# Regrouping a fused linear-attention and FFN kernel, with two more units transposed by DMA

## The chip, the cores and the metric

One core of one Trainium2 chip. The time is device microseconds (us) of one execution, median of several runs; the kernel before takes 233.85 us. A profile's span is about 2 us shorter than that time, because it starts with the first instruction and ends with the last.

In the lines of the profile PE is TensorE (PEld its weight loads), DVE is VectorE, ACT ScalarE, POOL GpSimd, and SPq SyncE's queue, which issues nearly all transfers.

## The reference, cut to what matters

A block-wise decaying linear attention over 4 batches, 8 heads, 768 positions and head width 64, and then a bilinear feed-forward network on its output, 3072 tokens wide 512:

```python
intra = einsum('bhic,bhjc->bhij', qb, kb) * Dmask;  intra = einsum('bhij,bhjd->bhid', intra, vb)
inter = einsum('bhid,bhde->bhie', qb * lam_pow, kv_state)
out[:, :, sl] = intra + inter
kv_state = lam_block * kv_state + einsum('bhsd,bhse->bhde', kb * rev_pow, vb)
# ... then, with x = out as (tokens, heads * width):
y = ((x @ w_a) * (x @ w_b)) @ w_out          # 512 -> 1536 -> 512, float32 out
```

## The kernel before

The 3072 tokens are 24 units of 128 tokens, and six units make a batch. Units are handled in groups. While TensorE runs the feed-forward matmuls of one group, the attention of later units is fitted between them by a hand-written plan: `PLAN[g]` lists pieces by slot. Slots 0 to 11 of a group are after each pair of projection halves, slots from 12 on after each half of a unit's output matmuls.

```python
GROUPS = (4, 1, 2, 4, 4, 4, 4, 1)
LOOKAHEAD = (3, 2)
DMA_T_FROM = 9                       # from this unit on q and k are transposed by DMA, before it on TensorE
PLAN = { ...
    2: [(0, "V", 6), (1, "T", 7), (1, "P", 8), (4, "T", 8), (4, "P", 9), (6, "S", 7),
        (6, "S", 8), (7, "V", 7), (6, "P", 10), (10, "V", 8),
        (12, "Q", (7, 8, 9, 10)), (12, "P", 11), (13, "V", 9), (14, "P", 12),
        (14, "O2", (9, 10))], ... }
```

The pieces: P prepares a unit (scales k and q on GpSimd, casts v, issues later loads), T transposes it on TensorE, S is scores and masks, V is the state update, O2 the outputs of two units, and Q the outputs of two units with the scores of two others between them. W stores a kept output: the outputs of the first seven units wait in SBUF and are stored later.

```python
    def prep_k(u):
        make_ks(u, "dve" if u < n0 + 2 else "pool")
        make_qs(u, "pool")
        used["u"] = u + 1
        if u >= DMA_T_FROM:
            qkT = qkT_pool.tile([128, 2, HP, 128], BF16, name="qkT", tag="qkT")
            nc.sync.dma_start_transpose(out=..., in_=...)          # cut
    def prep_v(u):
        make_vb(u, "pool" if u < n0 + 3 else "dve")
        pump()                                                     # issues the next loads, same queue
    def pieces_O(us, nxt=()):
        kqs = [score_banks() for u in nxt]
        for u in us: inter(u)
        for u, kq in zip(nxt, kqs): scores(u, kq)
        for u in us:
            intra(u); xT, col = xTs[u]; evac_o(u, xT, col)
        # ... state update beside, then masks(u, kq) on VectorE for each of nxt
```

The FFN of one group, with the special end of the very last unit, whose output goes out in three pieces:

```python
        for f in range(FC):
            a_sb = a_part(f, xT, gt)        # 4 matmuls of 128 * units columns, evicted by ScalarE
            b_part(f, xT, gt, a_sb, ab)     # 4 more; VectorE multiplies out of PSUM
            hook(f)
        for t in range(n):
            if last and t == n - 1:
                for lo, hi in ((0, 256), (256, 384), (384, 512)): ...   # out_mms, store of each piece
                return
            # out_mms in two halves with hooks, store(u0 + t, ...)
```

At the start TensorE runs idle matmuls, `warm(13, 512)`: 13 of 512 columns.

## Time and profile before

| | before |
|---|---|
| time, median of 5 | 233.85 us (233.6 to 234.01) |
| span of the profiled run | 231.8 us |
| first projection matmul to last matmul, TensorE | 209.88 us |
| last matmul's start to the end of the span | 3.31 us |

In the chain of waits a piece is "start, length, what"; when neighbouring pieces on TensorE (PE) touch, it issued without a hole. From 18.6 to 228.5 us that is so but for one wait of 0.34 us near 51 us. The lines are in the prediction. To add up TensorE's time I also took the start-to-start distance of every pair of neighbouring matmuls and subtracted the issue time of its kind (216, 109 and 56 ns for 512, 256 and 128 columns, 28.5 and 14.5 ns for the narrow attention kinds); what is left over is a wait or a mode switch (about 0.1 us, where TensorE goes between matmuls that use its whole array and the attention matmuls that use half of its rows or columns).

### The profile page before, as it was taken

How to read it: one execution, taken by the hardware profiler on the slowest of the kernel's cores; microseconds unless marked ns; L12 is line 12 of the kernel's file. 1: busy time of each engine (PE TensorE's matmuls, PEld its weight loads, DVE VectorE, ACT ScalarE, POOL GpSimd, SP SyncE). 2: the span in 40 equal slices, each digit the busy share in tenths (PEclk: the TensorE clock that was granted, in tenths of full speed). 3: DMA queues.
4: the chain of work that ended last, by engine and by line, in shares of the span. 5: the costliest groups of instructions: out<-in, count | busy, mean ns of one | idle time of the engine just before them, and what ended most of it. 6: DMA issues, size and time to landing. Idle time of an engine off the chain costs nothing.

```text
span 231.8 us, 4520 instructions
## 1 busy us (share of the span) xinstructions
PE 225.2 (97%) x1775; PEld 124.6 (54%) x1775; DVE 115.9 (50%) x204; ACT 91.1 (39%) x172; POOL 50.6 (22%) x65
## 2 busy tenths in 40 slices
PE   7799999999999999999999999999999999999994
PEld 2474444449698554454544454544454544444494
DVE  0896566636469726684334484235583323332050
ACT  3585754066463342333233332333332233332251
POOL 6070000248373333445000543001200000000000
PEclk9999999999999999999999999999999999999999
DMA  4999999999999999998759997229300220000311
GB/s 151 303 283 351 348 364 293 295 207 223 185 225 176 224 208 209 209 197 190 270 189 200 220 182 121 91 96 205 65 3 0 91 93 0 1 0 5 130 49 48
DMA packets 96389, 38.84 MB, mean 168 GB/s; under 512 B 83312, under 2 KB 91888, under 8 KB 96368
## 3 DMA queue, kind: packets, MB, share of 16 engines
q1 hardware_dynamic: 96224, 38.54, 72.9%
q8 instruction: 14, 0.23, 0.4%
q14 instruction: 7, 0.06, 0.1%
q10 hardware_dynamic: 144, 0.00, 0.0%
HBM read 28.32 MB, written 6.29 MB: 149 GB/s over the span
## 4 chain that ended last, share of the span: by engine, by line
PE 92%; DMA 3%; ACT 2%; SPq 1%; DVE 0%; issue 0%
PE a_ps L435 27%; PE b_ps L435 27%; PE op L467 27%; DMA k<-in_k_dram 3%; PE o_ps L352 3%; PE kq L310 2%; PE o_ps L342 2%; PE kvd L366 2%; PE tps L296 1%; ACT o_kept L458 1%; SPq L209 1%; PE kq L578 1%; ACT xT L359 0%; PE kv L366 0%; PE tk L542 0%; DVE scratch L531 0%
## 5 line engine op out<-in xcount | busy, mean ns | idle before, releaser
L447 DVE TENSOR_TENSOR ab<-a_sb,b_ps 128x512 bf16<-128x512 bf16 (+2 forms) x96 | 52.3, 552 | 77.9 <-PE b_ps L435 56.9
L435 PE MATMUL a_ps<-xT,wa_sb 128*128 128x512 bf16 (+2 forms) x384 | 77.2, 326 | 0.6 <-ACT xT L359 0.6
L435 PE MATMUL b_ps<-xT,wb_sb 128*128 128x512 bf16 (+2 forms) x384 | 77.2, 326 | 0.0
L442 ACT CAST a_sb<-a_ps 128x512 bf16<-128x512 f32 (+2 forms) x96 | 45.6, 481 | 63.1 <-PE a_ps L435 61.5
L467 PE MATMUL op<-wo_sb,ab 128*128 128x512 bf16 (+2 forms) x312 | 65.6, 363 | 0.0
L435 PEld LDWEIGHTS <-wb_sb 128*128 128x128 bf16 x384 | 34.5, 98 | 28.7
L435 PEld LDWEIGHTS <-wa_sb 128*128 128x128 bf16 x384 | 33.7, 98 | 29.1 <-POOL wa_sb L162 0.6
L467 PEld LDWEIGHTS <-ab 128*128 128x128 bf16 x312 | 28.8, 98 | 29.9
L327 DVE TENSOR_TENSOR m<-kq,lotri 128x512 bf16<-128x512 f32 x47 | 29.3, 682 | 18.1 <-PE kq L310 17.8
L259 POOL TENSOR_TENSOR qk<-kf,lp_k 128x512 bf16<-128x512 f32 x18 | 18.9, 1049 | 74.7 <-DMA kf<-in_k_dram 47.3
L264 POOL TENSOR_TENSOR qk<-qf,lp_q 128x512 bf16<-128x512 f32 x20 | 22.0, 1099 | 23.4 <-DMA qf<-in_q_dram 23.4
L462 ACT COPY o_sb<-op 128x512 f32<-128x512 f32 (+2 forms) x19 | 10.3, 541 | 34.0 <-PE op L467 34.0
L359 ACT CAST xT<-o_ps 128x512 bf16<-128x512 f32 x22 | 12.0, 590 | 17.9 <-PE o_ps L352 17.5
L398 DVE TENSOR_TENSOR st<-kvd,bdiag 128x512 bf16<-128x512 f32 x18 | 12.3, 682 | 4.9 <-PE kvd L366 3.8
L273 DVE CAST vb<-vf 128x512 bf16<-128x512 f32 x17 | 9.4, 553 | 0.0
L298 ACT COPY qkT<-tps 128x1024 bf16<-128x1024 bf16 x5 | 5.1, 1012 | 9.9 <-PE tps L296 9.9
L197 PE MATMUL idle<-idle_sb 128*128 128x128 bf16 (+1 forms) x31 | 7.2, 372 | 1.3 <-DVE idle_sb L192 1.3
L352 PE MATMUL o_ps<-m,vb 128*64 128x128 bf16 x192 | 7.9, 222 | 0.0
L273 POOL CAST vb<-vf 128x512 bf16<-128x512 f32 x7 | 4.7, 666 | 14.0 <-DMA vf<-in_v_dram 14.0
L342 PEld LDWEIGHTS <-st 128*128 128x128 bf16 x80 | 5.4, 98 | 2.8
L310 PE MATMUL kq<-qkT 64*128 64x128 bf16 x160 | 6.6, 218 | 0.0
L352 PEld LDWEIGHTS <-vb 128*64 128x64 bf16 x192 | 5.8, 109 | 1.4
(57 smaller groups left out, 87.4 us busy)
## 6 DMA issues: line engine op xcount, KB each, us to landing
vf<-in_v_dram SPq DMA_DIRECT2D x24, 256.0 KB, 4.9
qf<-in_q_dram SPq DMA_DIRECT2D x20, 256.0 KB, 4.4
kf<-in_k_dram SPq DMA_DIRECT2D x20, 256.0 KB, 4.6
out_dram<-o_sb SPq DMA_DIRECT2D x16, 256.0 KB, 2.0
wst<-in_moe_w_a_dram SPq DMA_DIRECT2D x6, 512.0 KB, 8.7
wst<-in_moe_w_b_dram SPq DMA_DIRECT2D x6, 512.0 KB, 8.8
wst<-in_moe_w_out_dram SPq DMA_DIRECT2D x6, 512.0 KB, 8.5
out_dram<-o_kept SPq DMA_DIRECT2D x7, 256.0 KB, 2.5
```

Source lines behind the costliest of these rows:

```text
L259: eng_of(eng).tensor_mul(qk[:, 1], raw.pop((u, "k")), lp_k[:, u % NB].to_broadcast([128, H, D]))
L264: eng_of(eng).tensor_mul(U[u]["qk"][:, 0], raw.pop((u, "q")), lp_q[:, u % NB].to_broadcast([128, H, D]))
L273: eng_of(eng).tensor_copy(vb, vf)
L310: nc.tensor.matmul(kq[i][:, hp, :], lhsT=d["kT"][p, hp, :], rhs=d["qT"][p, hp, :], start=True, stop=True, skip_group_check=True)
L327: nc.vector.tensor_mul(m, kq[i], lotri_bc)
L352: nc.tensor.matmul(d["o"][p, hp, :], lhsT=d["vb"][:, 2 * hp + i, :], rhs=d["m"](i, hp), start=(first and hp == 0), stop=True, skip_group_c ...
L359: nc.scalar.copy(xT[:, :, col:col + BLK], o_ps)
L398: nc.vector.tensor_mul(st[:].rearrange("p hp i d -> p hp (i d)"), ps[:].rearrange("p hp i d -> p hp (i d)"), bdiag_bc)
L435: nc.tensor.matmul(ps[:, :gt], lhsT=w_sb[:, s, f * 128:(f + 1) * 128], rhs=xT[:, s, :gt], start=(s == 0), stop=(s == KS - 1))
L442: nc.scalar.copy(a_sb[:, :gt], ps[:, :gt])
L447: nc.vector.tensor_mul(ab[:, f, :gt], a_sb[:, :gt], ps[:, :gt])
L467: nc.tensor.matmul(op[:, lo:hi], lhsT=ab[:, f, t * 128:(t + 1) * 128], rhs=wo_sb[:, f, lo:hi], start=(f == 0), stop=(f == FC - 1))
```

## The change

The intent: the early groups are made smaller, so that fewer units have to be ready early, while transfers are scarce. That makes room to transpose units 7 and 8 by DMA and take 16 transposes off TensorE. Kept outputs of the first seven units are stored a group later. The diff, cut to its core:

```diff
-GROUPS = (4, 1, 2, 4, 4, 4, 4, 1)
+GROUPS = (4, 1, 2, 2, 4, 4, 4, 3)
-DMA_T_FROM = 9
+DMA_T_FROM = 7
@@ PLAN
-    2: [(0, "V", 6), (1, "T", 7), (1, "P", 8), (4, "T", 8), (4, "P", 9), (6, "S", 7), ... cut
+    2: [(0, "V", 6), (1, "P", 8), (4, "P", 9), (9, "P", 10), (10, "S", 7), (10, "S", 8),
+        (11, "V", 7), (13, "P", 11), (14, "O2", (7, 8)), (15, "P", 12)],
+    3: [(1, "S", 9), (1, "S", 10), (2, "V", 9), (5, "Q", (9, 10, 11, 12)), (6, "P", 13),
+        (8, "V", 11), (9, "P", 14), (12, "O2", (11, 12))],
-PLAN[3] += [(_s, "W", None) for _s in range(12, 19)]
+PLAN[4] += [(_s, "W", None) for _s in range(9, 16)]
-PLAN[6] = [(4, "O", 23)]
+PLAN[6] = [(1, "P", 23), (4, "V", 21), (7, "Q", (21, 22, 23)), (12, "O", 23)]
-    qkT_pool = ctx.enter_context(tc.tile_pool(name="qkT", bufs=5))
+    qkT_pool = ctx.enter_context(tc.tile_pool(name="qkT", bufs=6))
-            elif c >= used["u"] + LOOKAHEAD[used["u"] > 9]:
+            elif c >= used["u"] + LOOKAHEAD[used["u"] > 8]:
... cut: the plans of the four-unit groups move by two units, the state update of unit 8 in 64-column form
```

## The prediction

> **What bounds the kernel now.** I read four views of the kernel before, in this order: the page's busy shares and slices, the chain of waits, the groups of instructions by form, and the DMA issues with the timeline of the transfer queue. The page first:
>
> ```profile
> span 231.8 us, 4520 instructions
> PE 225.2 (97%) x1775; PEld 124.6 (54%) x1775; DVE 115.9 (50%) x204; ACT 91.1 (39%) x172; POOL 50.6 (22%) x65
> DMA  4999999999999999998759997229300220000311
> ```
>
> PE is busy 97% of the span, DVE and ACT half or less. The DMA row is the second thing to see: nearly full for the first 18 of 40 slices (some 104 us), then slack. A busy PE need not be a full one, so I went to the chain of waits, whose pieces are PE start to start:
>
> ```profile
> by line: PE a_ps L435 31.9%; PE b_ps L435 29.0%; PE op L467 20.9%; PE kq L310 5.5%; PE o_ps L352 3.8%; PE kvd L366 3.0%; PE tps L296 3.0%; PE o_ps L342 3.0%; PE kvd L387 0.4%
> 67.38 0.44 PE b_ps L435 x4
> 67.81 0.45 PE tps L296 x8
> 68.26 0.44 PE a_ps L435 x4
> ...
> 70.01 0.55 PE kq L310 x16
> ...
> 84.69 0.86 PE b_ps L435 x4
> ```
>
> This window (62 to 92 us) covers what the change touches, and its chain names nothing but PE: each piece starts where the last one ends. Four 512-column matmuls take 0.86 us, four 256-column ones 0.44, and in the last group four 128-column ones:
>
> ```profile
> 220.68 0.22 PE a_ps L435 x4
> 226.04 2.66 PE op L467 x36
> ```
>
> So 216, 109 and 56 ns each: 53.3 ns per 128 columns plus about 2.5. The same chain between 46 and 62 us shows the one wait after the start that costs something, where group 1's first matmul waits for ACT's eviction of xT (group table: a_ps 0.5 us idle, released by ACT xT). From 52 to 226 us PE issues without a hole. The end is 11.3 us of a one-unit group, whose last output goes out in three pieces.
>
> **What the Trainium skill says.** "TensorE: Matmul & The Clock Gate", section "Back-to-back issue gap", gives N/2.4 + 2.5 ns for a warm matmul, which is 56, 109 and 216 ns here; it adds that in a real stream N=128 takes about 81 ns and N=512 about 131. This trace agrees with the formula (56, 109, 216) and not with those two figures. "TensorEngine Tiling (Array Packing)", section "Key Properties", says that changing the tiling mode drains TensorE. The trace shows it: the first matmul after a block of 64-row or 64-column matmuls is late by some 0.1 us (a_ps at 70.56 takes 0.54 in place of 0.44), so a scores block costs two such switches. "DMA: Bandwidth & Descriptors", section "Issuing engines are not separate DMA queues", says that all transfers run on the same 16 engines and interleave. So a DMA transpose competes with loads, and I read its cost from the transfers' landing times in the trace. "Perfetto Trace Analysis", section "Identifying the Most-Contended Engine", calls matmul busy time a bad metric because matmuls are pipelined; hence the start-to-start reading above.
>
> **The change part by part.**
>
> Regrouping, (4,1,2,4,4,4,4,1) to (4,1,2,2,4,4,4,3). The number of groups stays 8, so the weights of the two projections are run over 8 times in both: 96 matmuls per group, 12 wide output matmuls per unit. Only widths change: a 4-unit and a 1-unit group become a 2 and a 3. Per matmul 216 + 56 = 272 ns before. A 384-column matmul should take 160 + 2.5 = 162.5 ns (estimate from the three measured widths), and 162.5 + 109 = 271.5. Times 96, the gain is 0.05 us: nothing. One might have expected the one-unit group to be inefficient, but at 56 ns it isn't: PE needs 0.45 us per pair of halves, ACT 0.27 and DVE 0.29, and its 96 matmuls take 5.36 us without a hole. The tail is the same three pieces.
>
> Units 7 and 8 transposed by DMA. This removes 16 PE transposes at 56 ns: two pieces of 0.45, so 0.90 us off the path, every bit of it on PE's chain (the two tps pieces at 64.75 and 67.81). It also removes two ACT copies of 1.01 us, which are off the path (ACT 39% busy).
>
> Attention pieces in another order. From unit 7 on, before has 2 separate score pairs, 7 combined pieces with scores, one output pair and one single; after has 3, 6, 2 and 1. With switches of 96 + 120 = 0.22 us per score pair, 96 + 118 + 122 = 0.34 per combined piece, and 0.22 per output piece: before 0.43 + 2.35 + 0.44 = 3.22, after 0.65 + 2.02 + 0.65 = 3.32, so +0.10. The state update of unit 8 now runs in 64-column form: 0.12 in place of 0.22 (the pieces at 82.30 and 79.76), so -0.10. PE's instructions go from 1775 to 1763: minus 16, plus 4. Sum of these two: 0.
>
> Later stores of the 7 kept outputs: ordinary 256 KB stores, 2.5 us to landing, in a stretch where the DMA row has slack. Nothing on the path.
>
> One more transpose buffer and the earlier switch of the load lookahead from 3 to 2 units only serve the supply. Net of PE's own work: -0.05 - 0.90 + 0 = **about -0.95 us**, to 232.9.
>
> What may be given back is supply. Before, units 7 to 10 were all needed while the first two-unit group ran, to 83.8 us. After, that group has only 7 and 8 to prepare, and I add its length: 12 x 0.872 for the projections, 5.18 for 24 output matmuls, 0.66 for scores, 2 x 0.22 for state, 1.23 for outputs, so 18.0 us from 62.4 to 80.4. The next two-unit group then wants units 11 and 12 in its sixth slot: 80.4 + 6 x 0.872 + 0.66 + 0.22 = 86.5 us, and the transposed unit 12 after another 0.9, at some 87.4.
>
> When does unit 12 land? In the saturated stretch a load lands 1.2 us after the one before, a transpose about 0.9, and a load just behind a transpose about 1.5. Before, it landed at 86.1, having waited for POOL: its queue entry stood until POOL's product was ready.
>
> ```profile
> 68.19 4.64 SPq L282 DMA_TRANSPOSE qkT<-qk  x2
> ...
> 80.19 2.01 SPq L282 DMA_TRANSPOSE qkT<-qk  x1
> ```
>
> The waits of the queue itself say the same in sum (total, times, longest):
>
> ```profile
> SPq L282 <- POOL qk L264: 5.5, 7, 2.7
> ```
>
> After, the order of the queue is unit 9's v (lands 64.7 as before), transpose 7, loads of 10, transposes 8 and 9, loads of 11, transpose 10, loads of 12, transpose 11, loads of 13, transpose 12. That is 12 loads and 6 transposes: 8 x 1.2 + 4 x 1.5 + 6 x 0.9 = 21.0, so 85.7 at the earliest, and 87 to 88 if POOL's product (two products of 1.05 us after the load of k at about 79, so 81.1) or the queue's 2.1 us of issue holds it. Against 87.4 that is a wait of 0 to 0.6 us.
>
> A second small debt lies beside it. Four masks (2.47 us of DVE) now fall in slot 1 of a two-unit group, and the combined piece comes four slots later, not in the output phase. DVE after scores at 82.8: masks to 85.2, product 2 to 85.6, state copy to 86.2, products 3 and 4 to 87.0. The combined piece's output bank is the one that product 4 reads (of seven banks in turn), and PE arrives at 86.5: about 0.45 us of waiting. The two waits overlap. I put **+0.4 us** on both.
>
> Sum: 233.85 - 0.95 + 0.4 = **233.3 us**.
>
> **The rivals.** (a) No wait at all: all of 0.95 arrives, 232.9. For it: PE's queue had no hole before with a similar DVE load (four masks in slot 6, with no wait), and the regrouping spreads the demand. Against it: the 0.45 us worked out above. (b) The DMA supply fails by more: two further transposes in the full stretch push unit 12, or unit 11's v that DVE casts in order, several us late, and PE stands: 235 or more. For it: the DMA row at 9, and POOL's 47 us of waiting for k. Against it: most of POOL's waiting comes from running ahead, and the demand has been moved later. If units 13 on slid as well, they have 20 us in hand: their scores come at 107. (c) The smaller last group pays by a shorter tail, or a wider one by a better rate: some us. The rate of 56 ns at 128 columns speaks against it, and the tail is the same in both. (d) DVE becomes the bound in the two-unit groups: it was busy 14.8 of 21.4 us in the first one; after, the two together hold about the same work in 37 us. It speaks against.
>
> **Range and chances.** Best case is all of the PE saving and a little of the wait at 51.2 us: 232.5. A wait of 1.5 us makes 234.4. So 232.5 to 234.4 should hold 8 times in 10. Over 2% faster (under 229.2) would need five times what I find: 2%. Over 2% slower (over 238.5) needs a wait of 5 us: 3%. Within 2%: 95%.
>
> **What would show it.** In the profile after: transposes on PE 24 in place of 40; a 384-column form at some 162 ns start to start (four in 0.65 us in the chain); first 256-column matmul near 62.4 and the second two-unit group near 80.4; a hole of about 0.4 us on PE near 86.5, released by DVE's product or by the transpose into qkT; the last group from about 205 with the same three-piece end. I am wrong if the time moves by more than 1.5 us, if PE shows a hole of over 1 us past 52 us, if 384 columns cost other than 160 to 165 ns, or if the last group shows waits for ACT or DVE.

## The result, and the profile after

The changed kernel took 234.5 us (233.83 to 234.97, 5 runs). A ratio here is the mean time of one kernel's fast runs over that of the other's fast runs of the same rounds, so not quite the ratio of the medians. It was 1.0028 with a 95% interval of 1.0008 to 1.0048: slower by 0.3%, where a gain of 0.2% had been forecast, and just outside the range. The profile shown next is that of the slowest of the five runs (234.97), so its losses are larger than those of the median run; e12 gives a second profile.

The page of the changed kernel, same lines as before:

```profile
span 233.1 us, 4467 instructions
PE 222.7 (96%) x1742; PEld 127.7 (55%) x1763; DVE 116.6 (50%) x204; ACT 89.2 (38%) x170; POOL 50.2 (22%) x65
DMA  4999999999999999999999639990231000220012
```

The weight loads (PEld) count 1763, as foreseen; 21 matmul records are missing from the trace. TensorE's busy time fell by 2.5 us, in part because of those missing records, and the span rose by 1.3. The DMA row stays full to slice 22 (some 128 us) in place of slice 18.

The 384-column matmuls of the last group, in the chain of waits (start, length):

```profile
205.66 0.65 PE a_ps L433 x4
```

Four in 0.65 us are 162.5 ns each, as estimated. Up to 82 us TensorE keeps the forecast to 0.2 us: the first two-unit group starts at 62.5 us and the second at 80.55 (forecast 62.4 and 80.4). Then it leaves it. The chain of waits from 79 to 90 us:

```profile
76.80 4.50 DMA kf<-in_k_dram
...
81.46 1.04 POOL qk L257
82.50 1.19 POOL qk L262
...
83.71 5.06 DMA qkT<-qk
...
88.81 0.40 PE kq L308 x8
```

For the first time past the start the chain runs through a transfer. Unit 12's k lands at 81.3 us (I had reckoned 79), GpSimd makes its two products, the transpose is issued at 83.7 and lands at 88.77 (reckoned: 85.7 at the earliest, 87 to 88 likely), and only then can TensorE start the last eight scores. VectorE (DVE) in the same stretch, with the idle time before an instruction and what ended it in brackets:

```profile
82.32 0.47 DVE L271 CAST vb<-vf 128x512 bf16<-128x512 f32 x1 [2.27 <-DMA vf<-in_v_dram]
...
83.37 2.47 DVE L325 TENSOR_TENSOR m<-kq,lotri 128x512 bf16<-128x512 f32 x4
...
86.69 1.07 DVE L445 TENSOR_TENSOR ab<-a_sb,b_ps 128x256 bf16<-128x256 bf16 x3
```

It stood 2.27 us before the cast of unit 12's v, with the next group's products behind that cast in its queue. Then came four masks in one block, and products 3, 4 and 5 only at 86.7. What TensorE waited for in 62 to 100 us (total, times, longest; the idle time here leaves out the drain of the pipeline, so start to start it is 0.22, 0.60 and 0.58 us):

```profile
PE o_ps L340 <- DVE ab L445: 0.4, 1, 0.4
...
PE kq L308 <- DMA qkT<-qk: 0.4, 1, 0.4
PE a_ps L433 <- DVE ab L445: 0.2, 1, 0.2
```

The sums from start to start, in us, from the first projection matmul to the last matmul:

| | before | after | after minus before |
|---|---|---|---|
| feed-forward matmuls | 187.11 | 187.06 | -0.05 |
| transposes on TensorE | 2.24 | 1.34 | -0.90 |
| attention matmuls | 16.12 | 16.01 | -0.11 |
| mode switches, waits, rounding | 4.41 | 5.94 | +1.53 |
| sum | 209.88 | 210.35 | +0.47 |
| last matmul's start to the end | 3.31 | 4.26 | +0.95 |

The own work fell by 1.06, or 0.96 with one more switch; the waits near 82 to 89 us took 1.4 back. The rest, 0.95, is not on TensorE at all. It comes after the last matmul. The output stores from 226 us on, before (first line: issue times of the queue; second: from issue to landing, least, median, most):

```profile
L463 SPq DMA_DIRECT2D out_dram<-o_sb x3: 332/382/603, 227.8 to 229.0; - x3
...
DMA to landing us min/median/max: 1.7/1.8/2.0
```

and after:

```profile
L461 SPq DMA_DIRECT2D out_dram<-o_sb x4: 332/358/1537, 227.1 to 230.4; - x4
...
DMA to landing us min/median/max: 1.7/3.4/4.3
```

There is one store more at the end, the 256 KB of unit 22, issued at 227.08. It took 4.35 us to land, and the pieces behind it, issued at 228.18 and 228.75, took 3.5 and 3.2. In the trace's packet records something stands beside them (my table, not a view of the profile):

```
packets near the end (start us, bytes, ns)        before                     after
instruction fetch, one 16384 B packet             227.62  16384   945        228.19  16384  1714
unit 22's first 120 store packets, 2048 B each    -                          227.91 to 228.65, 81 to 93 ns each
unit 22's last 8 store packets                    -                          229.90 231 | 230.11 227 | 230.32 186 | 230.51 to 230.83, 84 to 85 each
```

Of the store's 128 packets 120 were through by 228.75. The last eight, a sixteenth of them, came from 229.90 on, when the fetch's packet ended (228.19 + 1.71). A first explanation: they are the share of one of the 16 DMA engines, and queued there behind the fetch. The packet records shown do not name the engine, so at this point it is a guess; it is tested below.

How this reaches the end of the program: the queue took 1.54 us to issue the third of these four stores (0.33 us in e5, where nothing is late). So the last piece, whose copy was done at 229.44, was issued at 230.38, 0.94 us later, and landed 1.73 us after that, as it does elsewhere. That is nearly all of the 0.95. Why the queue was held is not shown; the long issue ended at 230.28, 0.37 us after the fetch's packet.

### The profile page after: what moved, and what is told of

It is laid out like the page before. It is cut to its first block, busy times and chain, and to the rows that moved or that the text cites. A ratio compares the mean times of both kernels' runs of the same rounds, so it can differ in the third digit from the quotient of the medians.

```text
span 233.1 us, 4467 instructions
## 1 busy us (share of the span) xinstructions
PE 222.7 (96%) x1742; PEld 127.7 (55%) x1763; DVE 116.6 (50%) x204; ACT 89.2 (38%) x170; POOL 50.2 (22%) x65
## 4 chain that ended last, share of the span: by engine, by line
PE 85%; DMA 7%; SPq 2%; ACT 1%; issue 1%; POOL 1%; DVE 0%; POOLq 0%; ACTq 0%
PE a_ps L433 26%; PE b_ps L433 25%; PE op L465 24%; DMA k<-in_k_dram 3%; PE o_ps L350 3%; DMA qkT<-qk 2%; PE kq L308 2%; DMA kf<-in_k_dram 2%; PE o_ps L340 2%; PE kvd L364 1%; SPq L280 1%; ACT o_kept L456 1%; SPq L207 1%; PE tps L294 1%; POOL qk L262 1%
## 5 line engine op out<-in xcount | busy, mean ns | idle before, releaser
L445 DVE TENSOR_TENSOR ab<-a_sb,b_ps 128x512 bf16<-128x512 bf16 (+3 forms) x96 | 52.2, 551 | 75.3 <-PE b_ps L433 67.7
L433 PE MATMUL a_ps<-xT,wa_sb 128*128 128x512 bf16 (+3 forms) x377 | 76.6, 325 | 1.1 <-ACT xT L357 0.6
L433 PE MATMUL b_ps<-xT,wb_sb 128*128 128x512 bf16 (+3 forms) x382 | 77.0, 325 | 0.1
L440 ACT CAST a_sb<-a_ps 128x512 bf16<-128x512 f32 (+3 forms) x96 | 45.6, 480 | 66.1 <-PE a_ps L433 55.1
L465 PE MATMUL op<-wo_sb,ab 128*128 128x512 bf16 (+2 forms) x300 | 64.2, 362 | 0.9 <-issue 0.5
L433 PEld LDWEIGHTS <-wb_sb 128*128 128x128 bf16 x384 | 36.0, 98 | 26.6
L433 PEld LDWEIGHTS <-wa_sb 128*128 128x128 bf16 x384 | 35.3, 98 | 27.5 <-POOL wa_sb L160 0.6
L262 POOL TENSOR_TENSOR qk<-qf,lp_q 128x512 bf16<-128x512 f32 x20 | 21.5, 1077 | 23.0 <-DMA qf<-in_q_dram 23.0
L271 DVE CAST vb<-vf 128x512 bf16<-128x512 f32 x17 | 10.2, 597 | 3.2 <-DMA vf<-in_v_dram 3.2
L296 ACT COPY qkT<-tps 128x1024 bf16<-128x1024 bf16 x3 | 3.0, 1012 | 8.9 <-PE tps L294 8.9
```

Source lines behind the costliest of these rows:

```text
L262: eng_of(eng).tensor_mul(U[u]["qk"][:, 0], raw.pop((u, "q")), lp_q[:, u % NB].to_broadcast([128, H, D]))
L271: eng_of(eng).tensor_copy(vb, vf)
L433: nc.tensor.matmul(ps[:, :gt], lhsT=w_sb[:, s, f * 128:(f + 1) * 128], rhs=xT[:, s, :gt], start=(s == 0), stop=(s == KS - 1))
L440: nc.scalar.copy(a_sb[:, :gt], ps[:, :gt])
L445: nc.vector.tensor_mul(ab[:, f, :gt], a_sb[:, :gt], ps[:, :gt])
L465: nc.tensor.matmul(op[:, lo:hi], lhsT=ab[:, f, t * 128:(t + 1) * 128], rhs=wo_sb[:, f, lo:hi], start=(f == 0), stop=(f == FC - 1))
```

## The experiments

Theory A says that the waits near 87 us are the loss on TensorE, and that transfers cause them. Its rivals are VectorE's own backlog from the regrouping, and a loss that only moves. Theory F says that the slow end is the instruction fetch. Its rivals are a slow end that any three-unit last group has, and chance. Times are medians; the stretch is from the first projection to the last matmul, the tail from there to the end of the span. Without any wait but the one near 51 us, the changed kernel's stretch is 208.98 (measured in e6, e8 and e10).

| run | time | ratio to before (95%) | stretch | tail |
|---|---|---|---|---|
| after | 234.5 | 1.0028 (1.0008 to 1.0048) | 210.35 | 4.26 |
| after again (e12) | 234.42 | 1.0011 (0.9989 to 1.0033) | 209.92 | 4.16 |
| e1 Q in slot 8 | 233.77 | 0.9989 (0.9974 to 1.0003) | 209.37 | 4.28 |
| e2 units 7, 8 on TensorE | 233.98 | 1.0004 (0.9992 to 1.0016) | 210.62 | 3.08 |
| e3 old groups, DMA for 7, 8 | 234.06 | 1.0006 (0.9990 to 1.0021) | 210.79 | 3.12 |
| e4 last group 2 + 1 | 233.79 | 0.9994 (0.9982 to 1.0007) | 209.97 | 3.12 |
| e5 fetch shifted | 233.21 | 0.9972 (0.9955 to 0.9989) | 209.72 | 3.15 |
| e6 fetch shifted, pieces moved | 232.43 | 0.9937 (0.9918 to 0.9955) | 208.98 | 3.17 |
| e7 loads of v on ScalarE | 234.32 | 1.0028 (0.9998 to 1.0057) | 209.73 | 3.92 |
| e8 pieces moved | 233.15 | 0.9978 (0.9956 to 1.0000) | 208.98 | 3.71 |
| e9 before, other start | 233.44 | 0.9990 (0.9951 to 1.0028) | 209.89 | 3.22 |
| e10 as e6, kept outputs early | 232.46 | 0.9932 (0.9903 to 0.9960) | 208.98 | 3.16 |
| e11 as e5, cast of v 12 on GpSimd | 233.16 | 0.9962 (0.9930 to 0.9994) | 209.72 | 3.17 |

All gave correct results.

### e1: the combined piece three slots later

```diff
-    3: [(1, "S", 9), (1, "S", 10), (2, "V", 9), (5, "Q", (9, 10, 11, 12)), (6, "P", 13),
+    3: [(1, "S", 9), (1, "S", 10), (2, "V", 9), (6, "P", 13), (8, "Q", (9, 10, 11, 12)),
```

> The changed kernel with one edit: the combined piece that needs unit 12 (outputs of 9 and 10, scores of 11 and 12) moves from slot 5 to slot 8 of the second two-unit group. Theory A (the loss sits in TensorE's waits near 87 us: 0.60 us for an output bank that VectorE's product frees, 0.58 us for unit 12's transpose to land): both waits go, the wait of 0.22 us near 82.8 us stays, so 1.2 us faster than the changed kernel, about 233.3 us. Rival B (TensorE's order is not what costs; the loss is at the end of the program): no change, 234.5 us. Rival C (the debt only moves: the same masks and products now stand before the output matmuls): a new wait near 93 us and less than half of the gain.

Measured: the stretch fell by 0.98 us against the first profile of after, to 209.37, and the three waits were gone. Some 0.4 us of new waits stood at 92 us, behind the masks. The tail stayed at 4.28. So A holds for the place, and C has a part: 0.4 us of debt moved. The tail shows that the slow end does not come from this piece.

### e2: units 7 and 8 on TensorE again, the regrouping alone

```diff
-DMA_T_FROM = 7
+DMA_T_FROM = 9
-    2: [(0, "V", 6), (1, "P", 8), (4, "P", 9),
+    2: [(0, "V", 6), (1, "T", 7), (1, "P", 8), (4, "T", 8), (4, "P", 9),
```

> The changed kernel with units 7 and 8 transposed on TensorE again (the regrouping alone). Theory A (two more transposes push the transfer queue, and with it unit 12, 2.7 us later): TensorE gets 0.9 us more work, unit 12 lands at about 86 us and TensorE's waits near 82.8 and 88 us go (0.8 us); the wait for the output bank shrinks, as VectorE no longer waits 2.3 us for the values of unit 12. Sum about 0 to minus 0.4: 234.1 to 234.5 us. Rival (the waits come from the regrouping itself, VectorE's backlog of masks, not from the transfers): the waits stay and the time rises by 0.9 to 235.4 us.

Measured: 233.98 us, which is a little under A's range, but for another reason. Unit 12's transpose landed at 86.8 us (88.8 and 88.5 in the two profiles of after), and no wait for it is left. Yet the stretch was 210.62: take off the 0.90 of transposes, and 209.72 remains, still 0.74 above the kernel without waits. The chain of waits of this run shows whose debt that is:

```profile
85.14 1.05 DVE m L325 x2
...
87.26 0.75 DVE ab L445 x2
...
88.06 0.61 PE o_ps L340 x8
88.66 0.55 PE kq L308 x16
```

No transfer is in it. The masks of units 9 and 10, then product 4, then TensorE. So the rival has the larger part: VectorE's backlog, which comes with the regrouping, remains when the transfers are on time. What made the time good was the tail, 3.08 us, with the same three-unit last group. Its 16 more matmuls put the last fetch at 226.37 us, before unit 22's store.

### e3: the transposes alone, in the old groups

```diff
 (kernel before)
-DMA_T_FROM = 9
+DMA_T_FROM = 7
-    2: [(0, "V", 6), (1, "T", 7), (1, "P", 8), (4, "T", 8), (4, "P", 9), (6, "S", 7),
+    2: [(0, "V", 6), (1, "P", 8), (4, "P", 9), (6, "S", 7),
-    qkT_pool = ctx.enter_context(tc.tile_pool(name="qkT", bufs=5))
+    qkT_pool = ctx.enter_context(tc.tile_pool(name="qkT", bufs=6))
```

> The kernel before with units 7 and 8 transposed by DMA (that part alone, in the old groups). Theory A: TensorE saves 0.9 us, but units 7 and 8 are wanted at 68.5 us, and the second transpose lands at about 70.7 us or later; a wait of about 2 us takes the place of the saving, and unit 10, wanted at 76 us with a landing 2 to 3 us later than 74.9, adds up to 1 us. So slower than before by 1 to 2 us: 235 to 236 us. Rival (transfers have slack enough): all of the 0.9 us arrives, 232.95 us. The end of the program should be as before, 3.1 to 3.3 us from the last matmul's start to the end of the span.

Measured: one wait of 1.75 us for unit 8's transpose, in the waits of this run:

```profile
PEld L310 <- DMA qkT<-qk: 1.7, 1, 1.7
PE kq L310 <- DMA qkT<-qk: 1.6, 1, 1.6
```

The stretch rose by 0.91: 1.75 for 0.90 saved, with little else. The second wait that I had expected, for unit 10, did not come. The time was 234.06, under my 235 to 236. The tail was 3.12 and not 3.31, and the page counts one instruction fetch fewer than that of before:

```profile
q8 instruction: 13, 0.21, 0.4%
```

So the regrouping is what makes the DMA transposes possible, and without it they turn into a wait.

### e4: the last group as two and one

```diff
-GROUPS = (4, 1, 2, 2, 4, 4, 4, 3)
+GROUPS = (4, 1, 2, 2, 4, 4, 4, 2, 1)
-PLAN[6] = [(1, "P", 23), (4, "V", 21), (7, "Q", (21, 22, 23)), (12, "O", 23)]
+PLAN[6] = [(1, "P", 23), (4, "V", 21), (7, "Q", (21, 22, 23))]
+PLAN[7] = [(4, "O", 23)]
```

> The changed kernel with its last group of three cut in two and one (nine groups). Theory A (the end of the program costs 0.9 us more because the store of the unit before the last is in flight when the last unit's pieces are stored, beside an instruction fetch): the tail from the last matmul to the end goes back from 4.3 to 3.3 us, and 96 more matmuls cost 2.5 ns each, 0.24 us; sum 0.7 us faster than the changed kernel, 233.8 us. Rival B (the end's 0.9 us was chance in that one profiled run, the slowest of five): 0.24 us slower, 234.7 us.

Measured: 233.79 us for 233.8 expected, tail 3.12, and the 96 more matmuls cost 0.24 us. With one unit at the end no other store is in flight. This run alone does not tell the fetch from the stores, since its last fetch, at 222.09 us, lay elsewhere too.

### e5: only the instruction count changed

```diff
-    warm(13, 512)
+    warm(29, 230)
```

> The changed kernel with the 13 idle matmuls of 512 columns at the very start replaced by 29 of 230 columns (the same columns in all, 16 more matmuls and as many weight loads, while TensorE has nothing else to do). Nothing else on any engine changes order. Theory F (the slow end, 4.26 us from the last matmul to the end of the span, is a 16 KB instruction fetch that falls on the last stores; it falls where the count of TensorE's instructions puts it): the fetch comes some 2 us earlier, as with units 7 and 8 on TensorE, the tail goes to 3.1 us, and the time falls by 1.1 us, to 233.4 us. Rival G (a three-unit last group has a slow end by itself, because its stores come closely one after the other): the tail stays at 4.3 us and the time at 234.5 us.

Measured: 233.21 us, tail 3.15. The only edit is 16 more matmuls in the idle time at the start. The last fetch began at 224.61 us, and now the store issued just before that, unit 21's at 223.94, is the slow one. The stores of this run in 222 to 226.2 us:

```profile
L461 SPq DMA_DIRECT2D out_dram<-o_sb x1: 332/332/332, 223.9 to 223.9; - x1
...
DMA to landing us min/median/max: 3.7/3.7/3.7
```

and from 226.2 us on:

```profile
L461 SPq DMA_DIRECT2D out_dram<-o_sb x4: 332/332/333, 226.5 to 228.9; - x4
...
DMA to landing us min/median/max: 1.6/1.6/2.0
```

In after it is the other way round: the store at 224.49 landed in 2.0, the one at 227.08 in 4.35. The slow store moves with the fetch, from a place where the end waits for it to one where nobody does.

The other traces settle it. In twelve of the fourteen profiles a fetch of 16384 bytes began 0.67 to 1.47 us after the issue of a 256 KB store in the last 20 us; that store landed 3.23 to 4.38 us after its issue, and always 1.36 to 1.55 us after the fetch's packet had ended. The other 256 KB stores from unit 21 on took 2.00 to 2.04. So the store waits for the fetch. The slow end itself stands in all five profiles with 1763 weight loads (after, e12, e1, e7, e8) and in none of the five with 1779 (e2, e5, e6, e10, e11).

Counting the weight loads issued before each fetch shows why a small change in count moves it:

```
run                          weight loads in all   issued before the last three fetches
before                       1775                  1489 1611 1760
after                        1763                  1505 1612 1751
e2 (units 7, 8 on TensorE)   1779                  1486 1612 1743
e3 (old groups, DMA)         1759                  1361 1484 1612   (none after that)
e5 (29 idle matmuls)         1779                  1485 1612 1739
```

The trace of before has 14 fetches of this queue, 100 to 149 pairs of weight load and matmul apart after the second, 128 in the mean. The Trainium skill says the same ("Runtime: NRT & Kernel Launch", section "Instruction fetch mechanics"): instruction memory is refilled in blocks of 16 KiB, 256 instructions, by a DMA queue of the sequencer's own. It calls the cost mostly hidden; here it is hidden for TensorE, and not for a store that is in flight beside it, where it cost about 1 us at the end of the program. F holds and G falls.

### e6 and e8: the two pieces in the output phase, with and without the shift

```diff
-        ... (5, "Q", (9, 10, 11, 12)), (6, "P", 13), (8, "V", 11), (9, "P", 14), (12, "O2", (11, 12))],
+        ... (6, "P", 13), (8, "V", 11), (9, "P", 14), (12, "Q", (9, 10, 11, 12)), (14, "O2", (11, 12))],
-    warm(13, 512)        (e6 alone)
+    warm(29, 230)
```

> The changed kernel with 29 idle matmuls of 230 columns at the start, and with the combined piece moved to slot 12 and the output piece to slot 14 of the second two-unit group (the output phase, where the kernel before had them in its own two-unit group). If theories A and F hold, only the 0.34 us wait near 51 us is left, TensorE takes 208.9 us from the first projection to the last matmul (before 209.9), the tail is 3.1 us (before 3.3), so 1.2 us faster than before: 232.7 us, a ratio of 0.995. If either is wrong: 233.4 us or more.

> The changed kernel with the two pieces moved to slots 12 and 14, without the shifted instruction fetch. Theory A: waits of 0.60 and 0.58 us go, perhaps 0.22 more; TensorE's stretch falls from 210.35 to 209.0 us; the tail stays at 4.3 us if the fetch depends on the instruction count alone (theory F). So 233.2 us, and the tail is the difference to the kernel with both edits (1.1 us). Rival: the piece in the output phase makes the last products late and a new wait of 0.5 us or more stands before the next group.

Measured: e8 took 233.15 us with a stretch of 208.98 and a tail of 3.71 (expected 233.2, 209.0 and 4.3); e6 took 232.43 us with 208.98 and 3.17 (expected 232.7, 208.9, 3.1). All waits near 82 to 92 us are gone. Why e8's tail lies between the two kinds can be read in the traces: its fetch's packet was shorter (1.43 us, in after 1.71) and ended 2.40 us after the issue of unit 22's store. In e7, e12, after and e1 it ended 2.52, 2.72, 2.83 and 2.84 us after that issue, and the tails stand in the same order: 3.71, then 3.92, 4.16, 4.26 and 4.28. The chain of e6 around the moved piece has nothing but TensorE:

```profile
93.50 0.45 PE o_ps L340 x8
93.95 0.55 PE kq L308 x16
94.50 0.57 PE o_ps L350 x16
95.07 0.12 PE kvd L385 x8
```

Between output matmuls there is time for the masks: VectorE has no products to make there. e6 is the version that beats both kernels, by 0.6% against before with an interval clear of 1.

### e7: the loads of v on another queue

```diff
-        nc.sync.dma_start(out=t, in_=...)
+        (nc.scalar if w == "v" and 10 <= u <= 13 else nc.sync).dma_start(out=t, in_=...)
```

> The changed kernel with the loads of v of units 10 to 13 issued from ScalarE's queue in place of SyncE's; same bytes, same engines. It asks why unit 12 landed 2.7 us later than before. Theory I (each transpose holds the issuing queue for 2.1 to 2.5 us, and the queue's issue time is what is short): SyncE is freed of four issues of 0.6 to 0.9 us, and the transpose of unit 12 lands 2 to 3 us earlier, 86 to 87 us. Rival T (the 16 engines move about 200 GB/s in this stretch whatever is asked, and a transpose is 256 KB like a load, 1.3 us): it lands at 88.8 us as before, within 0.5. ScalarE may lose some time to the issues; the landing decides, not the time, which I expect at 234 to 235 us.

Measured: unit 12's transpose landed at 87.6 us. Theory I wanted 86 to 87; T wanted within 0.5 of 88.8. Neither fits to the letter, but eight other runs with the same order of transfers (e1, e4, e5, e6, e8, e10, e11, e12) had it at 87.8 to 88.5 us, so 87.6 is 0.2 below the earliest of those. The issue of the transposes of units 11 to 13 shrank to 1.23 to 1.25 us, from 2.1 to 3.0, and the landing hardly moved. I read this so: most of the issue time is the queue's being held up, and the rate of the 16 DMA engines is what is short. From unit 9's v to unit 12's transpose before moved 16 transfers of 256 KB in 21.35 us and after 18 in 23.81: 1.33 and 1.32 us each, 197 GB/s. I think the case is made for T, by the equal rate more than by this run.

### e9: control, the other start in the kernel before

```diff
 (kernel before)
-    warm(13, 512)
+    warm(29, 230)
```

> The kernel before with the same 29 idle matmuls of 230 columns at the start: a control. Theory F: its last fetch, at 227.6 us, already lies beside a one-unit tail with no store in flight, so only the small part of the tail goes, 3.31 to 3.1 us: 0.2 us faster than before or nothing, 233.6 to 233.9 us, and TensorE's stretch stays at 209.9 us. Rival: the other start itself makes things faster (a steadier clock): 0.5 us or more, which would then have to be taken off the gain of the kernel with both edits.

Measured: 233.44 us, ratio 0.999 with a wide interval, stretch 209.89, tail 3.22. The other start as such brings nothing on TensorE, so of e6's gain little or nothing is due to it.

### e10: the kept outputs one group earlier

```diff
 (e6)
-PLAN[4] += [(_s, "W", None) for _s in range(9, 16)]
+PLAN[3] += [(_s, "W", None) for _s in range(9, 16)]
```

> The kernel with both edits (29 idle matmuls, pieces in slots 12 and 14), and the seven kept outputs stored one group earlier again (slots 9 to 15 of the second two-unit group), the part of the change not tested yet. The transfers are full there at about 197 GB/s, so seven stores of 256 KB delay the loads behind them by some 9 us in all; units 13 and 14, whose scores come at about 105 us, landed at 93 and 98 us. Theory: they land 5 to 9 us later and TensorE waits 0 to 2 us: 232.4 to 234.5 us. Rival (nothing waits for it): 232.4 us, the same.

Measured: 232.46 us, stretch 208.98: the same as e6. The stores did push transfers back. The transposes of units 15 and 16 landed at 109.7 and 115.1 us, in e6 at 106.0 and 112.1. Nobody waited. This part of the change is neutral.

### e11: the cast that held VectorE, on GpSimd

```diff
 (e5)
-        make_vb(u, "pool" if u < n0 + 3 else "dve")
+        make_vb(u, "pool" if u < n0 + 3 or u == 12 else "dve")
```

> The changed kernel with 29 idle matmuls at the start, and the cast of unit 12's values on GpSimd in place of VectorE, which stood idle 1.8 to 2.3 us before that cast for its load and kept the products of the next group behind it. Theory A2 (the binding thing is the landing of unit 12's transpose; the wait for the output bank only stands in front of it): the bank wait falls from 0.35 us to under 0.1, and the wait for the transpose grows by about as much; the sum of the waits near 87 us stays at 0.5 to 0.7 and the time within 0.2 us of that kernel without the move, 233.2 us. Rival B2 (the two waits are separate debts that add): 0.35 to 0.5 us faster, 232.8 us.

Measured: 233.16 us, and the stretch of 209.72 is e5's to the hundredth. The time is A2's, but its mechanism isn't: the wait for the output bank stayed at 0.35 us in place of shrinking, the wait for the transpose fell from 0.21 to 0.08, and two waits for banks held by the next masks came (0.16 each). So neither expectation was right. The late v of unit 12 is not behind the 0.35 us. By the chain of waits the block of four masks is; no run changed the masks themselves. In e2, e5, e7 and e11, and in e4 after its extra matmuls, the debt is 0.74 or 0.75 us in all, whatever the transfers did. In e4 and e5 a wait for unit 12's transpose (some 0.3 and 0.2 us) is part of that sum, and the waits behind the next masks are smaller by as much.

### e12: the changed kernel once more

```diff
 (no edit)
```

> The changed kernel itself once more, for a second profile (its first was the slowest of five runs) and a ratio on another chip. Theory: VectorE's backlog costs 0.75 us in every run, as in the five variants with the piece in slot 5, whose TensorE stretch was 209.7 us; the waits for unit 12's loads and transpose are what varies, 0 to 0.65 us. So the stretch is 209.7 to 210.4 us, the tail 3.7 to 4.3 us, and the time 234 to 234.9 us, a ratio of 1.001 to 1.005. If the stretch is 210.3 again, the waits for transfers belong to every run; if the tail is 3.2, the fetch is chance and not set by the instruction count.

Measured: stretch 209.92, tail 4.16, 234.42 us. The bank wait was 0.37 and the one for unit 12's transpose 0.59 us. So the waits were 0.94 us here and 1.37 in the first profile: 0.74 of VectorE's, and in these two profiles 0.2 and 0.6 from late transfers on top. The tail is not chance. This ratio, 1.0011, does not by itself exclude 1; the two together say a little slower.

## Why the prediction was wrong

**What bounds the kernel, and TensorE's own work: right.** Own work was forecast at -0.95 us and measured at -0.90 (208.98 without waits against 209.88); added up piece by piece it is -0.96 (-0.05 for widths, -0.90 for transposes, 0 for the reordering). The regrouping by itself brings nothing on TensorE, as said: 162.5 ns at 384 columns.

**"The tail is the same three pieces": this step failed.** The pieces were the same, but not what flies beside them. It was sized at 0 and measured at +0.95 and +0.85 us in the two profiles. In the first profile that is as large as the miss on the waits (1.37 for 0.4), in the second it is the larger (0.94 for 0.4). With a one-unit last group the store before the pieces was issued 6.5 us earlier; with three units it is 1.1 us. An instruction fetch falls into that moment, the last piece is issued 0.9 us late, and e5 removes the cost by moving the fetch alone. I had looked at TensorE's end of the tail and not at the DMA's.

**"I put +0.4 us on both": right in kind and place, mis-sized.** 1.37 and 0.94 us were measured. The bank wait was seen rightly, at 0.45 (measured 0.35 without late transfers). What I left out is that the next block of masks is late too, which brings it to 0.74.

**"The two waits overlap": wrong.** One stands before the scores, the other in the middle of them, and TensorE pays them in turn: 0.60 and 0.58 in the first profile.

**"A transpose about 0.9": mis-sized.** I took it from single gaps between landings, though the trace of before already had 16 transfers in 21.35 us. In the full stretch a transpose costs what a load costs, 1.33 us, being 256 KB at 197 GB/s. The sum of 21.0 us for 18 transfers was 23.8, so unit 12 landed at 88.8 and 88.5 in place of 87 to 88.

**"In a stretch where the DMA row has slack": wrong, without cost.** The kept outputs now go out at 111 to 131 us, and the row is full to 128; they took 4.1 us to landing in the median and not 2.5. e10 shows that TensorE does not wait for them.

**The rivals.** (b), late transfers, was right in kind, but worth 0.6 and 0.2 us in the two profiles and nothing beyond VectorE's debt in e4, e5, e7 and e11. (d), VectorE as the bound, I dismissed by its mean load of 14.8 in 21.4 us; a mean says nothing about a block of 2.5 us in a group whose slots last 0.87. (c) had the wrong sign: the last group cost time at the end.

**The range** was 0.1 us short at the top. The sum fits for the first profile: -0.90 + 1.37 + 0.95 - 0.07 (first projection 0.07 us earlier) is +1.35, against +1.34 us of span. The medians differ by 0.65 only, since that profile is of the slowest run.

Left open: why the queue's issue of a store is held up to 1.5 us in the slow end, why the first three of the late packets go 0.2 us apart, and why the waits for transfers differ by 0.4 us between runs of the same kernel.

## What to carry to other kernels

When TensorE is full, count what a change takes off it, and then look for the debts at each place where another engine works in blocks: compare the block (four masks, 2.5 us) with the slot (0.87 us), not the mean loads. Where transfers are full, count bytes at the rate of that stretch, for a DMA transpose as for a load. Look at what is in flight in the last 5 us of a program, fetches too: a change of 16 idle matmuls at the start was worth 1 us at its end.

## What the Trainium skill lacked or had wrong

- "TensorE: Matmul & The Clock Gate", section "Back-to-back issue gap": its N/2.4 + 2.5 ns, which it gives for an isolated matmul, fits these streams with a weight load per matmul (56, 109, 162.5 and 216 ns at 128 to 512 columns); its sustained figures, 81 and 131 ns, do not.
- "TensorEngine Tiling (Array Packing)", section "Key Properties": no size is given for the drain at a mode switch; here 0.09 to 0.12 us each, 39 or 40 per run, 4.3 us in all.
- "Runtime: NRT & Kernel Launch", section "Instruction fetch mechanics": nothing on fetches slowing other transfers. A 256 KB store near the end with a fetch beside it took 3.2 to 4.4 us to land in place of 2.0, some 1.5 us from the end of the fetch's packet.
- "DMA: Bandwidth & Descriptors": nothing on loads and SBUF-to-SBUF transposes mixed. Here, in 256-byte packets, both ran at 197 GB/s, 1.33 us per 256 KB, and a transpose held its issuing queue for 1.2 to 3.8 us.
